# A Winograd convolution with batch norm and SiLU: the order of its opening written out as a table

## The chip, the cores and the metric

The kernel runs on one core of a Trainium2 chip. The metric is the device time of one execution in microseconds. Three timed runs of the kernel before gave 185.06, 185.35 and 185.8 us, median 185.35. PE is the matrix engine (TensorE), DVE the vector engine, ACT the scalar engine, POOL GpSimd, SP the engine that here only issues loads and stores.

## The reference

A 1-d convolution of width 3 over the sequence, per-channel scale and shift, and SiLU. x is [2, 2048, 1024] in bf16, w is [3, 1024, 1024].

```python
xp = jnp.pad(x, ((0, 0), (1, 1), (0, 0)))
y = sum(jnp.einsum('bsc,cd->bsd', xp[:, k:k + 2048, :], w[k]) for k in range(3))
inv_std = 1.0 / jnp.sqrt(var + 1e-5)
y = (y - mean) * (g * inv_std) + b
return y * jax.nn.sigmoid(y)
```

## The kernel before

**The method.** Six neighbouring outputs are computed from eight inputs with eight products instead of eighteen: the eight inputs are transformed to eight *points* (numbers 0 to 7; 0 is "point 0", 7 is "point inf"), each point is multiplied by a transformed weight, and the eight products are combined to six outputs. Points 0 and 7 take taps 0 and 2 of w as they are; points 1 to 6 take `u`, sums and differences of the taps, that POOL makes (lines 157 to 248): even sums `e0` to `e2`, then `u0` (points 1, 2), `u1` (3, 4), `u2` (5, 6). POOL's order is: the scales of the batch norm, which need the parameters `prm` (`scales`, line 239), the even sums and scaled copies (`evens`, 199), a doubled middle tap and the six `u` of output chunk 0 (`left`, 206), then those of output chunk 1.

**Transform jobs.** x comes in 2 sequences x 8 blocks of 128 channels ("chunks"), 512 KB each, the first two in two halves. A block has 16 frames. A *job* is six or four frames: as many matmuls of 168 columns (line 296: the x frame is the stationary side, the constant matrix `rm` the moving one) into two PSUM banks, and then one copy of 1008 or 672 elements per partition to `T_sb` by ACT (310) or DVE (312). A block is 6 + 6 + 4 frames. Each sequence has one *short* job more for its tail (eight matmuls of 48 columns, line 285, from the load `xl`).

**Products.** For each of 8 output chunks and 2 sequences there is a `Unit`: 8 points x 8 input chunks = 64 matmuls of 342 columns (line 340; in the first unit 470), copies on ACT and combines on DVE (356), SiLU on ACT (361), a store. The first unit (`First`, output chunk 0, sequence 0) uses banks 0 to 3 and mixes its products with the jobs of sequence 1: points 0, 7, 1, 3, 2 and 4, one point after the other, over 8 input chunks each. Points 0 and 7 are copied out to `kept`; point 1 is copied to `p`, point 2 is added in the same bank, and three combines make `sd`.

**The order of the work.** All engines execute in the order in which the program names their instructions. While the program is built, a small model keeps a `clock` per engine and estimated landings (lines 79 to 107, `landed`, `matmuls`, `busy`). The jobs of sequence 0 come first, all of them; `keep_busy` (99) adds filling matmuls where the model sees a gap (five of them, line 106). Then a loop (589) takes either the next job of sequence 1 or the next product of the first unit, by which one the model lets start first. Each job takes the pair of banks that is free first (`place`, 265): (4,5), (6,7), (2,3), for sequence 0 (0,1) as well. `ends` picks ACT or DVE for each copy (302, 479).

**Queues.** SP issues, in order: first halves of x blocks 0 and 1, the tail `xl`, x block 2, taps 0 and 2 of w, blocks 3 to 7, tap 1, the second tail, sequence 1's eight blocks, the next weights. ACT issues `rm`, the two second halves and `prm` (line 560, 8 KB in 128 pieces of 64 bytes). The loads of blocks 6 and later wait for one of six buffers.

Of the kernel before, what the change touches and what calls it, by code (L numbers as in the profile page):

```python
# [18 lines left out]
WARM_AT = 7000.0  # L19
FILL = 9000.0  # L20
# [3 lines left out]


@with_exitstack
def kernel(
# [50 lines left out]

    clock = {"pe": 4150.0, "act": 3700.0, "dve": 1500.0, "pool": 7000.0, "dma": 2300.0}
    cost = {"act": (0.833, 170.0), "dve": (1.042, 155.0), "pool": (2.0, 80.0)}  # L80

    def ends(e, size, ready):
        return max(clock[e], ready) + cost[e][0] * size + cost[e][1]

    def busy(e, size, ready=None):
        clock[e] = ends(e, size, clock["pe"] + 250.0 if ready is None else ready)
        return clock[e] + 100.0

    def landed(nbytes):
        left = nbytes  # L90
        slow = max(0.0, 6100.0 - clock["dma"]) * 300.0
        at = min(left, slow)
        clock["dma"] += at / 300.0 + (left - at) / 410.0
        return clock["dma"] + 300.0

    def matmuls(cols):
        clock["pe"] += cols / (2.34 if clock["pe"] > WARM_AT else 1.18)

    def keep_busy(until, bank):


        z = zeros.bitcast(BF16)
        n, gap, left = (192, 200.0, 100.0) if clock["pe"] < FILL else (384, 900.0, 600.0)
        if clock["pe"] + gap < until:
            while clock["pe"] + left < until:
                nc.tensor.matmul(ps[:, bank, 0:n], lhsT=z[:, 0:P], rhs=z[:, 0:n], start=True, stop=True)  # L106
                matmuls(n)

    xt, xt_at, raw, raw_at = {}, {}, {}, {}
    small, small_at = {}, {}  # L110

    def load_small(bi):
        t = xlpool.tile([P, CT * P], BF16, name="xl")
        nc.sync.dma_start(out=t[0:LROWS], in_=xl[bi])
        small[bi], small_at[bi] = t, landed(LROWS * CT * P * 2)

    def load_x(bi, ct, parts=1):
        t = xpool.tile([P, NF, P], BF16, name="xw")
        xt[bi, ct], xt_at[bi, ct] = t, []
        step = NF // parts  # L120
        for q in range(parts):
            s = slice(q * step, (q + 1) * step)
            (nc.scalar if q else nc.sync).dma_start(out=t[:, s], in_=x[bi, ct, :, s])
            at = landed(P * step * P * 2)
            xt_at[bi, ct] += [at] * step

    def load_w(dc, taps):
# [7 lines left out]
        for k in taps:  # L135
            raw_at[dc, k] = landed(P * CT * P * 2)
# [52 lines left out]
    def pool(n=1):  # L189
        clock["pool"] += n * 2130.0  # L190
        return clock["pool"]

    u_at = {}

    def prepare_first(dc):
# [3 lines left out]
        def evens():  # L199
            clock["pool"] = max(clock["pool"], raw_at[dc, 0], raw_at[dc, 2])  # L200
# [3 lines left out]
            pool(4)  # L204

        def left():
            clock["pool"] = max(clock["pool"], raw_at[dc, 1])
            double_w(dc, nc.gpsimd)
            pool(0.5)
            for q, i in ((0, 0), (1, 0), (0, 1), (1, 1), (2, 0), (2, 1)):  # L210
                transform_w(dc, q, (i,))
                u_at[1 + 2 * q + i] = pool()
# [39 lines left out]
    t_at, bank_free = {}, {}  # L252

    class Jobs:


        def __init__(self, bi):
            self.bi = bi
            self.todo = [(ct, f, min(6, NF - f)) for ct in range(CT) for f in range(0, NF, 6)]
            self.todo.insert(6, (None, 0, 0))  # L260

        def __bool__(self):
            return bool(self.todo)

        def place(self):

            ct, f, nf = self.todo[0]
            slots = [(4, 5), (6, 7), (2, 3)]
            if not self.bi:
                slots += [(0, 1)]  # L270
            slot = min(slots, key=lambda s: max(bank_free.get(k, 0.0) for k in s))
            at = small_at[self.bi] if ct is None else xt_at[self.bi, ct][f + nf - 1]
            return slot, max([at] + [bank_free.get(k, 0.0) for k in slot])

        def do(self):
            slot, at = self.place()
            clock["pe"] = max(clock["pe"], at)
            bank = slot[0]
            ct, f, nf = self.todo.pop(0)
            T = T_sb[self.bi]  # L280
            if ct is None:
                size, count, slot = CT * NJ * LAST, CT, slot[:1]
                src = ps[:, bank, 0:size].rearrange("p (c j n) -> p c j n", j=NJ, n=LAST)
                for c in range(CT):
                    nc.tensor.matmul(
                        src[:, c], lhsT=small[self.bi][0:LROWS, c * P:(c + 1) * P], rhs=rm[0:LROWS, :, 0:LAST],
                        start=True, stop=True,
                    )
                src = src.rearrange("p c j n -> p (c j) n")
                dst = T[:, :, :, NT:NB].rearrange("p c j n -> p (c j) n")  # L290
            else:
                size, count = nf * NJ * WT, nf
                per = nf // 2
                src = ps[:, bank:bank + 2, 0:per * NJ * WT].rearrange("p b (f j n) -> p b f j n", f=per, j=NJ)
                for q in range(nf):
                    nc.tensor.matmul(  # L296
                        src[:, q // per, q % per], lhsT=xt[self.bi, ct][:, f + q], rhs=rm, start=True, stop=True
                    )
                src = src.rearrange("p b f j n -> p j b f n")
                dst = T[:, ct, :, f * WT:(f + nf) * WT].rearrange("p j (b f n) -> p j b f n", b=2, f=per)  # L300
            matmuls(size)
            e = min(("act", "dve"), key=lambda k: ends(k, size, clock["pe"] + 250.0))
            done = busy(e, size)
            for k in slot:
                bank_free[k] = done
            if ct is None or f + nf == NF:
                for c in range(CT) if ct is None else (ct,):
                    t_at[self.bi, c] = max(done + 50.0, t_at.get((self.bi, c), 0.0))
            if e == "act":
# [14 lines left out]
    class Unit:  # L324
# [20 lines left out]
        def copy(self, q, dst=None, by=None):  # L345
# [6 lines left out]
            busy("act", self.hi - self.lo)  # L352
            return dst

        def combine(self, out, in0, scalar, in1, op1=ALU.add):
            nc.vector.scalar_tensor_tensor(out=out, in0=in0, scalar=scalar, in1=in1, op0=ALU.mult, op1=op1)  # L356
            busy("dve", (self.hi - self.lo) * (2 if len(out.shape) > 2 else 1))

        def silu(self, rows, src):
# [5 lines left out]
            busy("act", (self.hi - self.lo) * (2 if len(src.shape) > 2 else 1))  # L365
# [69 lines left out]
    class First(Unit):  # L435
# [3 lines left out]
        def __init__(self, dc, bi):  # L439
# [14 lines left out]
        def at(self):  # L454

            j, q, _, ct = self.todo[0]
            u = raw_at[self.dc, 0 if j == 0 else 2] if j in (0, NJ - 1) else u_at[j]
            if q == 2 and jobs[1]:
                return float("inf")
            return max(u, t_at[self.bi, ct], bank_free.get(q, 0.0))  # L460

        def do(self):
            at = self.at()
            j, q, add, ct = self.todo.pop(0)
            clock["pe"] = max(clock["pe"], at)
            if j == 0 or j == NJ - 1:
                lhsT = raw[self.dc][:, 0 if j == 0 else 2, ct]
            else:
# [3 lines left out]
                start=not add and ct == 0, stop=ct == CT - 1, skip_group_check=add,  # L472
            )
            matmuls(NB)
            if ct == CT - 1:
                bank_free[q] = self.behind(j, q)

        def out_of(self, q, dst, by=1.0):
            e = min(("act", "dve"), key=lambda k: ends(k, NB, clock["pe"] + 250.0))
            if e == "act":  # L480
# [3 lines left out]
            return busy(e, NB)  # L484

        def behind(self, j, q):
            b0, b1 = self.bank[:2]
            sd = self.sd
            if j == 0 or j == NJ - 1:
                return self.out_of(q, self.kept[:, j and 1])  # L490
            if j in (1, 3, 5):
                self.p = getattr(self, "p", {})
                self.p[j] = cpool.tile([P, NB], FP32, name="pc")
                return self.out_of(q, self.p[j], 4.0 if j == 3 else 1.0)
            if j == 2:
                at = self.out_of(q, sd[:, 0])
                self.combine(sd[:, 1], b1, 1.0, self.kept[:, 0])
                self.combine(sd[:, 2], self.p[1], 2.0, b1, ALU.subtract)
                at = max(at, clock["dve"])
                self.combine(sd[:, 3], sd[:, 2], 1.0, self.kept[:, 1])  # L500
                return at
            if j == 4:
                self.combine(b1, b0, -2.0, self.p[3])
                for t, a, s in zip(self.t, (-0.0125, -0.05, -0.2), (sd[:, 1:3], sd[:, 0:3:2], sd[:, 0:4:3])):
                    self.combine(t, self.low, a, s)
                return clock["dve"]
            return clock["dve"]
# [50 lines left out]
    load_x(0, 1, 2)  # L558
    load_small(0)
    nc.scalar.dma_start(out=prm, in_=prm_in)  # L560
# [13 lines left out]
    scales()  # L574
# [137 lines left out]
```

## Time and profile before

| what | us |
|---|---|
| median of the timed runs | 185.35 |
| the profiled execution | 185.1 |
| its span (first to last instruction) | 183.0 |
| around the span | 2.1 |
| PE busy | 175.1 |
| DVE busy | 152.1 |
| POOL busy | 141.6 |
| ACT busy | 108.8 |

The span is what the trace shows; the 2.1 us around it lie outside the trace. Times in rows of the trace count from the start of the span. In a row of the order of time, the first number is the start, the second the length, `x38` the number of instructions, and the bracket the idle time before it with what ended it. In the rows of stretches, the columns are PE, PEld (weight loads, which overlap), DVE, ACT and POOL busy time, the granted TensorE clock, the DMA share and GB/s. In the chain of waits a row is start, length, engine, tile and line.

### The profile page before, as it was taken

How to read it: one execution, taken by the hardware profiler on the slowest of the kernel's cores; microseconds unless marked ns; L12 is line 12 of the kernel's file. 1: busy time of each engine (PE TensorE's matmuls, PEld its weight loads, DVE VectorE, ACT ScalarE, POOL GpSimd, SP SyncE). 2: the span in 40 equal slices, each digit the busy share in tenths (PEclk: the TensorE clock that was granted, in tenths of full speed). 3: DMA queues.
4: the chain of work that ended last, by engine and by line, in shares of the span. 5: the costliest groups of instructions: out<-in, count | busy, mean ns of one | idle time of the engine just before them, and what ended most of it. 6: DMA issues, size and time to landing. Idle time of an engine off the chain costs nothing.

```text
span 183.0 us, 3476 instructions
## 1 busy us (share of the span) xinstructions
PE 175.1 (96%) x1371; PEld 125.1 (68%) x1371; DVE 152.1 (83%) x192; ACT 108.8 (59%) x174; POOL 141.6 (77%) x77
## 2 busy tenths in 40 slices
PE   7988899999999999999999999999999999999992
PEld 5876778766666666666666666666666666668891
DVE  0479577899978999999998999887998899766690
ACT  3789688846754565455545654564547454564773
POOL 2199999999999779999999999999999976000000
PEclk9999999999999999999999999999999999999997
DMA  5999991080308130543055304630302020203042
GB/s 177 370 415 372 412 416 77 19 326 4 129 0 260 46 129 0 136 171 129 0 113 192 129 0 79 225 129 2 123 9 114 15 101 33 91 38 126 6 180 80
DMA packets 7200, 24.58 MB, mean 134 GB/s; under 512 B 1072, under 2 KB 1456, under 8 KB 7184
## 3 DMA queue, kind: packets, MB, share of 16 engines
q1 hardware_dynamic: 6464, 23.73, 35.7%
q10 hardware_dynamic: 720, 0.64, 1.1%
q8 instruction: 10, 0.16, 0.4%
q14 instruction: 6, 0.05, 0.1%
HBM read 14.93 MB, written 9.44 MB: 133 GB/s over the span
## 4 chain that ended last, share of the span: by engine, by line
PE 62%; DVE 24%; DMA 7%; issue 2%; ACT 2%; DVEq 0%; ACTq 0%
PE ps L340 54%; DMA xw<-in_x_dram 7%; DVE ps L356 7%; DVE t L356 6%; PE ps L296 5%; DVE e L165 5%; PE ps L470 2%; DVE T_sb L312 2%; DVE sd L356 2%; DVE f L356 2%; ACT T_sb L310 1%; ACT yh L361 1%; PE ps L106 0%; ACTq L68 0%; DVEq L701 0%
## 5 line engine op out<-in xcount | busy, mean ns | idle before, releaser
L340 PE MATMUL ps<-T_sb,u 128*128 128x342 bf16 (+2 forms) x768 | 109.7, 298 | 0.0
L340 PEld LDWEIGHTS <-u 128*128 128x128 bf16 x768 | 72.5, 97 | 32.7
L172 POOL TENSOR_TENSOR u<-e,w1x 128x1024 bf16<-128x1024 f32 x32 | 69.3, 2189 | 3.9 <-DVE e L165 3.7
L340 PE MATMUL ps<-T_sb,wch 128*128 128x342 bf16 (+2 forms) x256 | 39.8, 299 | 0.5 <-DVE ps L356 0.4
L172 POOL TENSOR_TENSOR u<-e,wch 128x1024 bf16<-128x1024 f32 x16 | 38.8, 2439 | 0.5
L356 DVE SCALAR_TENSOR_TENSOR t<-ps,sd 128x684 f32<-128x684 f32 (+2 forms) x49 | 37.5, 819 | 0.6
L361 ACT ACTIVATE yT<-ps,beta,scale 128x342 bf16<-128x342 f32 (+1 forms) x42 | 29.2, 728 | 11.4 <-PE ps L340 11.4
L312 DVE CAST T_sb<-ps 128x1008 bf16<-128x1008 f32 (+2 forms) x22 | 22.6, 1066 | 11.7 <-PE ps L296 11.6
L340 PEld LDWEIGHTS <-wch 128*128 128x128 bf16 x256 | 24.2, 97 | 11.8 <-issue 1.2
L349 ACT COPY pc<-ps 128x342 f32<-128x342 f32 (+2 forms) x32 | 13.6, 425 | 30.4 <-PE ps L340 30.3
L310 ACT CAST T_sb<-ps 128x1008 bf16<-128x1008 f32 (+1 forms) x28 | 24.1, 892 | 5.5 <-PE ps L296 5.1
L356 DVE SCALAR_TENSOR_TENSOR ps<-ps,t 128x684 f32<-128x684 f32 (+2 forms) x32 | 26.5, 829 | 0.5
L165 DVE SCALAR_TENSOR_TENSOR e<-wch 128x1024 f32<-128x1024 bf16 x12 | 26.8, 2237 | 0.0
L296 PE MATMUL ps<-rm,xw 128*128 128x168 bf16 x256 | 23.4, 243 | 2.6 <-DMA xw<-in_x_dram 2.1
L296 PEld LDWEIGHTS <-xw 128*128 128x128 bf16 x256 | 20.2, 100 | 6.0 <-DMA xw<-in_x_dram 3.5
L356 DVE SCALAR_TENSOR_TENSOR ps<-ps,pc 128x342 f32<-128x342 f32 (+2 forms) x34 | 16.8, 495 | 8.5 <-PE ps L340 6.1
L159 POOL TENSOR_TENSOR e<-wch 128x1024 f32<-128x1024 bf16 x8 | 18.9, 2366 | 0.1
L361 ACT ACTIVATE yT<-t,beta,scale 128x684 bf16<-128x684 f32 x15 | 14.4, 959 | 0.0
L356 DVE SCALAR_TENSOR_TENSOR t<-ps,t 128x684 f32<-128x684 f32 (+2 forms) x17 | 13.9, 817 | 0.0
L349 ACT COPY sd<-ps 128x342 f32<-128x342 f32 (+2 forms) x16 | 6.8, 428 | 10.3 <-PE ps L340 9.7
L351 ACT ACTIVATE pc<-ps 128x342 f32<-128x342 f32 (+2 forms) x16 | 7.0, 438 | 8.9 <-PE ps L340 5.3
L356 DVE SCALAR_TENSOR_TENSOR sd<-pc,ps 128x342 f32<-128x342 f32 (+2 forms) x17 | 8.2, 483 | 4.5 <-ACT sd L349 4.4
(41 smaller groups left out, 66.2 us busy)
## 6 DMA issues: line engine op xcount, KB each, us to landing
out_dram<-yT SPq DMA_DIRECT2D x15, 576.0 KB, 2.8
xw<-in_x_dram SPq DMA_DIRECT2D x14, 512.0 KB, 7.5
wch<-in_w_dram SPq DMA_DIRECT2D x7, 768.0 KB, 5.6
wch<-in_w_dram SPq DMA_DIRECT2D x3, 256.0 KB, 4.9
xw<-in_x_dram SPq DMA_DIRECT2D x2, 256.0 KB, 3.6
xw<-in_x_dram ACTq DMA_DIRECT2D x2, 256.0 KB, 4.7
out_dram<-yh SPq DMA_DIRECT2D x1, 256.0 KB, 2.1
out_dram<-yh SPq DMA_DIRECT2D x2, 128.0 KB, 1.7
```

What stands on the lines that cost most here:

```text
L159: nc.gpsimd.tensor_tensor(sums[dc, q], a, b, op=ALU.add)
L165: nc.vector.scalar_tensor_tensor(out=e, in0=f, scalar=4.0, in1=h, op0=ALU.mult, op1=ALU.add)
L172: nc.gpsimd.tensor_tensor(wts[dc, q][:, i], sums[dc, q], o, op=(ALU.add, ALU.subtract)[i])
L296: nc.tensor.matmul(src[:, q // per, q % per], lhsT=xt[self.bi, ct][:, f + q], rhs=rm, start=True, stop=True)
L310: nc.scalar.copy(dst, src)
L312: nc.vector.tensor_copy(dst, src)
L340: nc.tensor.matmul(self.bank[q], lhsT=lhsT, rhs=T_sb[self.bi][:, ct, j, nsl], start=not add and ct == 0, stop=ct == CT - 1, skip_group_che ...
L349: nc.scalar.copy(dst, self.bank[q])
L351: nc.scalar.mul(dst, self.bank[q], by)
L356: nc.vector.scalar_tensor_tensor(out=out, in0=in0, scalar=scalar, in1=in1, op0=ALU.mult, op1=op1)
L361: nc.scalar.activation(self.yT[:, rows, self.y0:self.y0 + self.hi - self.lo], src, ACT.Silu, bias=beta[:, dc:dc + 1], scale=scale[:, dc:dc ...
L470: nc.tensor.matmul(self.bank[q], lhsT=lhsT, rhs=T_sb[self.bi][:, ct, j, :], start=not add and ct == 0, stop=ct == CT - 1, skip_group_check ...
```

## The change

The model that chose the order is taken out, with `keep_busy`, `place` and `ends`. In its place stands a table: each token is a job with its banks (A: 4,5; B: 6,7; C: 2,3; D: 0,1) and its copying engine (a: ACT, d: DVE), a short job (`s`), filling matmuls (`z5`) or a number of products of the first unit.

```diff
+BANKS = {"A": 4, "B": 6, "C": 2, "D": 0}
+ORDER = (
+    "Aa Ba Cd Da Ad Ba s2d z5 Dd Ba Ad Ca Bd Aa Dd Ca Aa Bd Ca Dd Aa Bd Ca 5 Ad 1 Bd Ca 5 Aa Cd 2 Ba "
+    "3 Aa Cd Ba 7 s4d Ca Bd Aa 4 Ca 1 Bd Aa 3 Ca 2 Ad Ba 2 Ca 2 Bd Aa 2 Ca 2 Ad Ba 2 Ca 3 Ba 1 Aa 1"
+)
+COPIES = {0: "d", 7: "a", 1: "d", 3: "d", 2: "d", 5: "a"}
...
-    jobs = [Jobs(0), Jobs(1)]
-    while jobs[0]:
-        slot, ready = jobs[0].place()
-        keep_busy(ready, slot[0])
-        jobs[0].do()
...
+    second = list(prepare_second(1))
+    second.pop(0)()
+    jobs, unit = Jobs(), First(0, 0)
+    for token in ORDER.split():
...
+        elif token[0] == "s":
+            jobs.do_short(int(token[1]), token[2])
+        elif token[0] in BANKS:
+            jobs.do(BANKS[token[0]], token[1])
         else:
-            unit.do()
+            for _ in range(int(token)):
+                unit.do()
+    for f in unit.later:
+        f()
+    while unit.todo[0][0] != 6:
+        unit.do()
+    second.pop(0)()
```

Points 0 and inf are now taken together, chunk by chunk (0 and 7 of chunk 0, then of chunk 1), and the first eleven of their sixteen products stand among the last jobs of sequence 0, behind chunk 6 and between chunk 7's jobs; the other five among chunk 0 of sequence 1. The other points follow as before. The combines behind points 2 and 4 are put off to the end of the table (`later`), and ACT's scaled copy of the next weights (`second.pop(0)`, which stood between jobs) behind them:

```diff
-            self.todo = [
+            self.todo = [(j, q, False, ct) for ct in range(CT) for j, q in ((0, 0), (NJ - 1, 1))] + [
                 (j, q, add, ct) for j, q, add in (
-                    (0, 0, False), (NJ - 1, 1, False), (1, 1, False), (3, 0, False), (2, 1, True), (4, 0, True),
-                    (5, 2, False), (6, 2, True),
+                    (1, 1, False), (3, 0, False), (2, 1, True), (4, 0, True), (5, 2, False), (6, 2, True),
                 ) for ct in range(CT)
             ]
```

Point inf is added to twice point 1 straight from the bank, before point 2 is added there; the later combine then subtracts the bank:

```diff
+            if j == 1:
+                self.combine(sd[:, 3], b1, 2.0, self.kept[:, 1])
             if j == 2:
-                at = self.out_of(q, sd[:, 0])
-                self.combine(sd[:, 1], b1, 1.0, self.kept[:, 0])
-                self.combine(sd[:, 2], self.p[1], 2.0, b1, ALU.subtract)
-                at = max(at, clock["dve"])
-                self.combine(sd[:, 3], sd[:, 2], 1.0, self.kept[:, 1])
-                return at
+                self.out_of(j, q, sd[:, 0])
+                self.later += [
+                    lambda: self.combine(sd[:, 1], b1, 1.0, self.kept[:, 0]),
+                    lambda: self.combine(sd[:, 2], self.p[1], 2.0, b1, ALU.subtract),
+                    lambda: self.combine(sd[:, 3], sd[:, 3], 1.0, b1, ALU.subtract),
+                ]
```

Of the first unit's copies out of PSUM, those of points 0, 1, 2 and 3 are now on DVE, those of 5 and inf on ACT (before: one on DVE, five on ACT). Of the 48 jobs and two short ones DVE now copies 20 and ACT 30 (before 22 and 28); of sequence 1 DVE has seven of six frames and the short one. And the parameters are loaded third on SP's queue instead of fourth on ACT's, with the scales named right behind:

```diff
     load_x(0, 0, 2)
     load_x(0, 1, 2)
+    nc.sync.dma_start(out=prm, in_=prm_in)
     load_small(0)
-    nc.scalar.dma_start(out=prm, in_=prm_in)
+    scales()
```

More of the change, by code (lines that the diff above doesn't have):

```diff
@@ L76 @@
     nc.vector.memset(dummy, 0.0)
[L79 to L110, printed above, removed]
+    xt, raw, small = {}, {}, {}
     def load_small(bi):
@@ new lines, in do_short @@
+        def do_short(self, bank, eng):
+            bi = self.short.pop(0)
+            src = ps[:, bank, 0:CT * NJ * LAST].rearrange("p (c j n) -> p c j n", j=NJ, n=LAST)
+            for c in range(CT):
+                nc.tensor.matmul(
+                    src[:, c], lhsT=small[bi][0:LROWS, c * P:(c + 1) * P], rhs=rm[0:LROWS, :, 0:LAST],
+                    start=True, stop=True,
+                )
+            dst = T_sb[bi][:, :, :, NT:NB].rearrange("p c j n -> p (c j) n")
+            self.out(dst, src.rearrange("p c j n -> p (c j) n"), eng)
```

131 lines of the change are left out of this document (30 added, 101 removed).

## Prediction

> **What bounds the kernel now.** I read the page first, then the busy time by stretches, then the chain of waits, then the order of time of TensorE (PE) from 10 to 37 us.
>
> ```profile
> span 183.0 us, 3476 instructions
> PE 175.1 (96%) x1371; PEld 125.1 (68%) x1371; DVE 152.1 (83%) x192; ACT 108.8 (59%) x174; POOL 141.6 (77%) x77
> ...
> L296 PE MATMUL ps<-rm,xw 128*128 128x168 bf16 x256 | 23.4, 243 | 2.6 <-DMA xw<-in_x_dram 2.1
> ```
>
> PE is the bound, but its busy time overlaps itself: the last row says 243 ns for a transform matmul, and below the next one starts after 72. So dead time must be found by counting starts. The stretches show where to look:
>
> ```profile
> 10.00:15.00 5.00, 4.21 (x53) 3.57 (x51) 4.33 (x4) 4.54 (x7) 4.48 (x8) 1.00 1.02 409
> 15.00:20.00 5.00, 3.71 (x47) 3.27 (x45) 4.11 (x5) 3.74 (x5) 4.85 (x3) 1.00 1.04 377
> 20.00:25.00 5.00, 5.00 (x60) 4.12 (x58) 3.02 (x4) 3.93 (x6) 5.00 (x4) 1.00 1.03 410
> ...
> 35.00:40.00 5.00, 5.00 (x38) 3.39 (x36) 4.93 (x7) 2.83 (x6) 4.92 (x3) 1.00 0.74 275
> ...
> 45.00:50.00 5.00, 5.00 (x37) 3.36 (x35) 4.95 (x7) 3.88 (x7) 4.92 (x3) 1.00 0.29 118
> ```
>
> The reader sees PE (first column) short of 5.00 before 20 us while the DMA share is 1.0: the loads of x hold it there. After 20 us PE is full. The chain of waits gives PE's price per matmul, and shows how the rest of the run goes:
>
> ```profile
> 26.12 0.89 PE ps L296 x10
> ...
> 27.00 0.58 PE ps L470 x4
> 27.58 0.43 PE ps L296 x6
> ...
> 50.39 4.82 PE ps L340 x32
> ...
> 79.71 93.97 PE ps L340 x664
> ```
>
> A product (342 columns) costs 0.58/4 = 0.145 us, a transform matmul (168 columns) 0.43/6 = 0.072 us. The chain passes from DVE to PE at 50.39 and for the last time at 79.71, and from there it is 664 products at 93.97/664 = 0.1415 us, so whatever PE gains by then reaches the end. Now PE itself:
>
> ```profile
> 10.70 3.29 PE L296 MATMUL ps<-rm,xw 128*128 128x168 bf16 x38 [0.48 <-DMA xw<-in_x_dram]
> 14.23 3.50 PE L296 MATMUL ps<-rm,xw 128*128 128x168 bf16 x42 [0.23 <-DVE T_sb L312]
> 19.00 1.04 PE L296 MATMUL ps<-rm,xw 128*128 128x168 bf16 x12 [1.27 <-DMA xw<-in_x_dram]
> ...
> 24.94 0.45 PE L470 MATMUL ps<-T_sb,wch 128*128 128x342 bf16 x2
> 25.47 1.53 PE L296 MATMUL ps<-rm,xw 128*128 128x168 bf16 x16
> ...
> 35.11 1.18 PE L470 MATMUL ps<-T_sb,u 128*128 128x342 bf16 x7
> ```
>
> The row at 14.23 holds the last 42 transform matmuls of sequence 0 (128 in all). After it PE has nothing that it may do until block 0 of sequence 1 lands: 1.27 us idle at 19.00, which is the largest hole in the run. At 25.47 it lost another 25.47 - 24.94 - 2x0.145 = 0.24 us to a PSUM bank that had not been emptied, and 0.22 inside that row to another (the chain has its last ten from 26.12, and the six before them need 0.43 of the 0.65). The last product of point 4 starts at 35.11 + 6x0.145 = 35.98, so ends its turn at 36.13.
>
> **The change part by part.**
>
> *Order table.* The work on PE is the same: 48 transform jobs, two short ones, 48 first products, and the same five filling matmuls. What moves is that 11 products of points 0 and inf now stand between the last jobs of sequence 0. They need T of chunks 0 to 5 and taps 0 and 2 of w:
>
> ```profile
> 1.61 0.42 SPq L114 DMA_DIRECT2D xl<-in_xl_dram  x1
> 2.08 0.42 SPq L123 DMA_DIRECT2D xw<-in_x_dram  x1
> 3.99 0.81 SPq L134 DMA_DIRECT2D wch<-in_w_dram  x2
> ```
> ```profile
> 2.12 0.45 ACTq L560 DMA_DIRECT2D prm<-in_prm_dram  x1
> ```
> ```profile
> wch<-in_w_dram SPq DMA_DIRECT2D x3, 256.0 KB, 4.9
> ...
> prm<-in_prm_dram ACTq DMA_DIRECT2D x1, 8.0 KB, 6.1
> ```
>
> The second tap is issued about 4.4 and takes 4.9, so both are in at 9.3. At 14.23 there are 26 matmuls to the end of chunk 6 (16.1), then 11 products (1.60) and chunk 7's 16 matmuls (1.16): 18.9, against 19.0 for the block that PE waits for. The bank waits inside the row at 14.23 (3.50 less the 0.17 by which a matmul's 243 ns outlasts its turn, less 42x0.072 = 0.3) may push it to 19.1. The hole is filled.
>
> From 19.0 on both orders are counts. Before: 128 matmuls 9.2, the short job 0.2, 48 products 6.96: 35.4; the trace says 36.13, so 0.7 was lost, 0.45 of it in the two bank waits. After: 37 products, 5.37, so 33.8; with the 0.25 that has no name kept, **34.05, or 2.1 us earlier**. If the bank waits stay as they are it is 1.6, if nothing is lost at all 2.3. I take **2.0**, since 0.1 may be carried past 19.0.
>
> That holds if nothing is late in the new order. Four covers:
>
> *Weights for points 1 to 4* come from POOL:
>
> ```profile
> 8.26 0.20 POOL L243 TENSOR_SCALAR sc<-prm 128x8 f32<-128x8 bf16 x1 [6.70 <-DMA prm<-in_prm_dram]
> ...
> 11.37 2.12 POOL L159 TENSOR_TENSOR e<-wch 128x1024 f32<-128x1024 bf16 x1
> ...
> 21.10 2.14 POOL L172 TENSOR_TENSOR u<-e,wch 128x1024 bf16<-128x1024 f32 x1
> ...
> 27.37 6.30 POOL L172 TENSOR_TENSOR u<-e,w1x 128x1024 bf16<-128x1024 f32 x3
> 33.63 2.12 POOL L159 TENSOR_TENSOR e<-wch 128x1024 f32<-128x1024 bf16 x1
> ```
>
> The first u is ready at 23.2. The table (Aa Cd 2 Ba 3 Aa Cd Ba) puts 32 transform matmuls (2.3) and 5 products (0.7) between 19.0 and the first product that wants it, so PE is there at 22.0. Unmoved, PE would stand 1.2 us. But POOL starts only when prm has landed (2.12 + 6.1 = 8.2), and then needs 11.37 - 8.26 = 3.1 us for the scales. *prm third on SP's queue* takes the place that xl had (issued 1.61):
>
> ```profile
> DMA to landing us min/median/max: 4.6/6.3/8.0
> ```
>
> These are xl's two loads; the smaller is the first, so it landed at 6.2. With prm at 6.2 or sooner the scales end by 9.3, as the second tap lands. POOL then starts 2.0 us earlier, and as it is busy without a break (5.00 of 5.00 above) all its u come 2.0 earlier: 21.2 against 22.0 wanted, then every 2.1 us (23.3, 25.4, 27.5) against about 24.5, 27.2, 30.7. Slack 0.8 at the first. SP's xl and x block 2 go out 0.42 later (one issue); a megabyte stands ahead of them in a stream at 409 GB/s, so nothing. ACT issues one DMA less before a first job that waits for PE anyway: nothing.
>
> *Blocks of x.* After 19.0 they land every 512 KB/410 GB/s = 1.28 us; PE reaches them in 1.6 to 1.9 us steps, so only the first is waited for. *Emptying the banks:*
>
> ```profile
> L310 ACT CAST T_sb<-ps 128x1008 bf16<-128x1008 f32 x17 | 16.9, 1001 | 5.2 <-PE ps L296 5.0
> ...
> L310 ACT CAST T_sb<-ps 128x672 bf16<-128x672 f32 x11 | 8.0, 725 | 0.3 <-PE ps L296 0.2
> ```
> ```profile
> 24.42 3.34 ACT L310 CAST T_sb<-ps 128x1008 bf16<-128x1008 f32 x4 [0.79 <-PE ps L296]
> ```
> ```profile
> 24.86 1.21 DVE L312 CAST T_sb<-ps 128x1008 bf16<-128x1008 f32 x1 [0.93 <-PE ps L296]
> 25.98 0.51 DVE L483 TENSOR_SCALAR kept<-ps 128x342 f32<-128x342 f32 x1
> ```
>
> (The first two rows group ACT's jobs from 4 to 37 us.) Of sequence 1 ACT has 9 jobs of six frames (1.00) and 8 of four (0.725) and one copy (0.5): 15.3 at most, and less what neighbours overlap, since two of each take 3.34 and not 3.45 in the row at 24.42, and with it 0.1 at best per job, 13.6 to 14.8. It can use 19.6 to 34.9, 15.3 us. DVE has 7 jobs (1.21), the short one (no more than a job), four copies and a combine (0.5 each): 12.2. Both fit; ACT's margin is 5 to 10%. ACT's scaled copy of the next weights moves behind the last job, to about 35.5, and POOL wants it after one more e and two u, 31.6 + 2.1 + 4.2 = 37.9: nothing.
>
> *Point inf from PSUM.*
>
> ```profile
> 35.71 0.50 DVE L356 SCALAR_TENSOR_TENSOR sd<-ps,kept 128x342 f32<-128x342 f32 x1
> ...
> 36.66 1.67 DVE L356 SCALAR_TENSOR_TENSOR sd<-sd,kept 128x342 f32<-128x342 f32 x1
> ...
> 55.71 0.52 DVE L356 SCALAR_TENSOR_TENSOR ps<-ps,pc 128x342 f32<-128x342 f32 x1 [2.07 <-PE ps L340]
> ```
>
> The combine with both inputs in SBUF took 1.67; its two replacements each read PSUM, as the 0.50 row does. So 1.67 goes and 1.0 comes (bounds: 0.5 to 1.67 each, so -0.7 to +1.7 on DVE), with three more copies (0.51 each) taken from ACT. DVE is full from 35 to 50 and only at 55.71 waits for PE (2.07), so it matters whether it keeps up: its last job now is chunk 6's second, behind which PE has 20 transform matmuls and 7 products (2.45), so PE ends it at 31.6 and DVE is free for the combines at about 32.9 instead of 35.7, 2.8 earlier for a PE 2.0 earlier. Cost on the path: nothing. POOL's next weights move by the same 2.0 as PE's need.
>
> **Sum:** 185.1 (the profiled execution: 183.0 span and 2.1 around it) less 2.0 is 183.1. The median of the runs, 185.35, lies 0.25 above that execution; halfway between the two bases I forecast **183.2**. The bounds of the unknown terms (1.6 to 2.3, and the base) give 182.8 to 183.7.
>
> **The rivals.** A measurement of this kernel can tell about 0.5%, 0.93 us, from no change.
>
> *A. prm does not land early enough.* If it lands at 8.2 as now, u is ready at 23.2, PE stands 1.2 at 22.0, and the time is 184.3. For it: 6.1 us from issue to landing for 8 KB. Against: xl's 4.6 from the very place. The Trainium skill (DMA: Bandwidth & Descriptors, "Issuing engines are not separate DMA queues") says that loads from SP and ACT run on the same 16 engines and interleave, and another issuing engine saves only issue time; by that rule the new queue brings only the half microsecond of earlier issue. That half microsecond (2.12 to 1.61) worked out in rows: landing 7.7, u at 22.7, PE stands 0.7, 183.8. No row here parts the queue from the time of issue; but xl, issued 0.5 before prm, landed 2.0 before it, so a place in the stream is worth more than its issue time. I put A at 184.0, between the two.
>
> *B. Banks.* ACT's margin is 5 to 10%. If waits like the 0.24 and 0.21 recur four times instead of twice, 0.9 of the gain is gone: 184.0. For: a fixed engine per job can't give way. Against: points 0 and inf keep PE off the banks for 0.3 to 0.7 us between jobs.
>
> *C. PE's fixed order meets a late u: slower.* All that stands behind point 1's first seven products (the second short job and the 18 jobs of chunks 2 to 7) waits with them; before, the first products that need a u stand near 27 (the row at 27.00), 3.8 after it is ready. Price 1:1. The gain is gone when the first u comes at 22.0 + 2.0 = 24.0, and from 25.0 the kernel is over 0.5% slower; at 25.2 it would take 186.4. That needs prm at over 10, beyond every row but xl's second load, 8.0 us in the full stream. Against: 6.2.
>
> *D. It is given back.* PE comes 2.0 earlier but DVE's work, full from 35 to 53.6, does not; PE then waits at 50.39, and the time is 185.1. For: 4.95 of 5.00. Against: the 2.8 above.
>
> **How the numbers follow.** Forecast 0.66, better than its range 0.03, A 0.10, B 0.10, D 0.06, C 0.05. The range takes in the forecast's bounds, A and B: 182.6 to 184.4. Faster by over 0.5% (under 184.4): forecast, the better end, B and most of A, 0.87; within: D and the rest of A, 0.08; slower: C, 0.05.
>
> **What would show it.** In the profile after: at 19 PE's wait for x under 0.3 instead of 1.27; POOL's first e at about 9.3 instead of 11.37 and its first u at 21.2; no PE idle at 22; the last product of point 4 near 34 instead of 36; no combine of 1.67; the hole before PE's 50.39 no larger than now. An idle PE at 22 with the u as its releaser says A or C, many short ones released by ACT B, one near 48 released by DVE D.

## The result, and the profile after

The changed kernel takes 183.08 us (median of 5 runs, 182.91 to 183.24), the kernel before on the same chip 185.17 (5 runs, 184.89 to 185.80): 2.1 us less, ratio 0.988 (95% interval 0.986 to 0.990). The forecast was 183.2. The profiled execution took 183.18 us with a span of 181.3; the one of before had 185.1 and 183.0. The spans of the five runs after are 181.0 to 181.5. In several kernels below the spans spread less than the times (in run 1 182.9 to 183.5 against 184.72 to 186.12), so I use them beside the times. A few executions, whatever the kernel, show a granted clock of 0.991 or less instead of 0.994 or more and a span 1.5 to 2.4 us longer; four of the twelve of run 6 are such.

The head of the page, after:

```profile
span 181.3 us, 3481 instructions
PE 174.4 (96%) x1371; PEld 124.5 (69%) x1371; DVE 151.6 (84%) x194; ACT 108.7 (60%) x173; POOL 141.4 (78%) x77
```

PE's share is the same 96%, DVE and POOL do what they did. A page's head can't show a gain of this kind, since the work is unchanged and only PE's idle time went. The stretches (the first column of busy time is PE's) say where:

```profile
10.00:15.00 5.00, 3.68 (x45) 3.26 (x46) 4.05 (x5) 3.85 (x5) 4.85 (x3) 1.00 1.03 419
15.00:20.00 5.00, 4.97 (x57) 4.15 (x55) 4.65 (x5) 3.34 (x5) 4.85 (x5) 1.00 1.04 376
...
35.00:40.00 5.00, 5.00 (x37) 3.35 (x35) 4.45 (x7) 4.12 (x7) 5.00 (x3) 1.00 0.79 298
```

Between 15 and 20 us PE is now busy for 4.97 instead of 3.71. Between 10 and 15 it is busy for less than before (3.68 against 4.21): in this execution the blocks of x came later. From 35 to 40 DVE, 4.93 before, has 0.55 to spare. Now PE itself, in order of time:

```profile
11.10 3.20 PE L225 MATMUL ps<-rm,xw 128*128 128x168 bf16 x38 [1.15 <-DMA xw<-in_x_dram]
14.52 2.13 PE L225 MATMUL ps<-rm,xw 128*128 128x168 bf16 x26 [0.21 <-ACT T_sb L242]
...
18.54 0.89 PE L389 MATMUL ps<-T_sb,wch 128*128 128x342 bf16 x5
19.46 1.04 PE L225 MATMUL ps<-rm,xw 128*128 128x168 bf16 x12
...
22.59 1.18 PE L389 MATMUL ps<-T_sb,u 128*128 128x342 bf16 x7
...
34.55 1.48 PE L389 MATMUL ps<-T_sb,u 128*128 128x342 bf16 x9
```

Block 0 of sequence 1 is the row at 19.46. The bracket of 1.27 us that stood there is gone. A bracket shows idle time after the last matmul's modelled end, so I also count starts: five products from 18.54 need 5 x 0.145 = 0.72, which leaves 0.20 to 19.46; before, the same count gave 1.44 (the row at 14.23 ends its last turn at 14.23 + 3.50 - 0.17 = 17.56). The first products that want a u (22.59) wait for nothing, and the two bank waits near 25 to 26 are not there. They had carried no bracket before either, so here too the count of starts decides: from 22.59 to 34.55 it leaves no gap over 0.1 us, against 0.24 and 0.22. The first of the nine products at 34.55 is the last of point 4, so that point ends at 34.70, where it ended at 36.13: **1.43 earlier**.

The span is 1.7 shorter, so 0.3 more was gained behind this point. The chain of waits has the place:

```profile
48.12 0.80 DVE ps L287
48.96 123.01 PE ps L272 x864
```

Before, the chain passed from DVE to PE twice, at 50.39 and at 79.71. Now it does so once, and 864 products follow in one piece. By the count of starts a hole of 0.30 stood at 79.71; it is gone, and 1.43 + 0.30 = 1.73 is the span's difference. The hole at 48.96 is 0.33, as it was at 50.39.

POOL and DVE, in order of time:

```profile
6.08 0.20 POOL L204 TENSOR_SCALAR sc<-prm 128x8 f32<-128x8 bf16 x1 [4.52 <-DMA prm<-in_prm_dram]
...
9.91 2.12 POOL L131 TENSOR_TENSOR e<-wch 128x1024 f32<-128x1024 bf16 x1 [0.78 <-DMA wch<-in_w_dram]
...
19.64 2.13 POOL L144 TENSOR_TENSOR u<-e,wch 128x1024 bf16<-128x1024 f32 x1
...
53.55 4.22 POOL L144 TENSOR_TENSOR u<-e,wch 128x1024 bf16<-128x1024 f32 x2
```
```profile
26.72 0.50 DVE L287 SCALAR_TENSOR_TENSOR sd<-ps,kept 128x342 f32<-128x342 f32 x1
...
34.47 0.50 DVE L287 SCALAR_TENSOR_TENSOR sd<-sd,ps 128x342 f32<-128x342 f32 x1
...
56.77 2.08 DVE L137 SCALAR_TENSOR_TENSOR e<-wch 128x1024 f32<-128x1024 bf16 x1
```

prm is there at 6.1 instead of 8.2, and POOL then stands 0.78 for the second tap of w, which is what limits it now. The combine of 1.67 became two of 0.50.

### The profile page after: what moved, and what is told of

The parts are those of the page before. It is cut to its first block, busy times and chain, and to the rows that moved or that the text cites. A ratio compares the mean times of both kernels' runs of the same rounds, so it can differ in the third digit from the quotient of the medians.

```text
span 181.3 us, 3481 instructions
## 1 busy us (share of the span) xinstructions
PE 174.4 (96%) x1371; PEld 124.5 (69%) x1371; DVE 151.6 (84%) x194; ACT 108.7 (60%) x173; POOL 141.4 (78%) x77
## 4 chain that ended last, share of the span: by engine, by line
PE 85%; DVE 6%; DMA 5%; ACT 1%; issue 0%; ACTq 0%; DVEq 0%
PE ps L272 71%; PE ps L225 8%; DMA xw<-in_x_dram 5%; PE ps L389 5%; DVE ps L287 3%; DVE t L287 3%; ACT yh L291 1%; ACT T_sb L242 1%; ACTq L76 0%; DVEq L618 0%; PE ps L233 0%; DVE sd L287 0%; DVEq L287 0%
## 5 line engine op out<-in xcount | busy, mean ns | idle before, releaser
L242 ACT CAST T_sb<-ps 128x1008 bf16<-128x1008 f32 (+1 forms) x30 | 25.2, 884 | 6.9 <-PE ps L225 6.3
L244 DVE CAST T_sb<-ps 128x1008 bf16<-128x1008 f32 (+2 forms) x20 | 21.2, 1086 | 9.3 <-PE ps L225 8.6
```

Source lines behind the costliest of these rows:

```text
L242: nc.scalar.copy(dst, src)
L244: nc.vector.tensor_copy(dst, src)
```

## The experiments

Two theories stood at the start. **Mine**: the gain is the hole at 19, filled by products, and the move of prm is worth nothing by itself but is the cover that lets the new order run (u in time). **The rival**: the parts help separately, or the stream of x (which differs from one execution to the next) or point inf's combine makes the time. The table has all runs; a kernel's ratio is to the kernel before on the same chip.

| run | kernel | time, us (runs) | span, median | ratio (95%) |
|---|---|---|---|---|
| 1 | changed, prm back behind ACT's two halves of x | 184.89 (12) | 183.0 | 0.9985 (0.9959 to 1.0011) |
| 2 | before, prm third on SP | 185.13 (12) | 183.2 | 0.9994 (0.9960 to 1.0029) |
| 3 | changed, products 0/inf behind block 0's first jobs | 184.66 (12) | 182.8 | 0.9971 (0.9943 to 0.9999) |
| 4 | changed, old combine of point inf | 183.24 (4) | 181.3 | 0.9883 (0.9838 to 0.9928) |
| 5 | changed, again | 183.11 (6) | 181.25 | 0.9875 (0.9834 to 0.9915) |
| 6 | changed, prm third on ACT | 184.03 (12) | 182.25 | 0.9939 (0.9903 to 0.9976) |
| 7 | changed, small load behind block 0 | 183.05 (6) | 181.0 | 0.9873 (0.9836 to 0.9909) |
| 8 | changed, one more copy on POOL | 184.00 (7) | 182.2 | 0.9921 (0.9891 to 0.9951) |
| 9 | changed, DVE's first e with one input | 182.97 (6) | 181.15 | 0.9868 (0.9836 to 0.9900) |
| 10 | run 8, DVE's first e with one input | 183.56 (6) | 181.75 | 0.9899 (0.9873 to 0.9925) |
| 11 | run 1, DVE's first e with one input | 184.26 (6) | 182.5 | 0.9930 (0.9906 to 0.9954) |
| 12 | run 7, DVE's first e moved | 183.70 (6) | 181.8 | 0.9918 (0.9900 to 0.9935) |

The kernel before took 185.23, 185.34, 185.37 and 185.19 beside runs 1 to 4, 5 to 8, 9 to 11 and 12, with median spans of 183.3 to 183.4.

### Run 3: the hole back

```diff
-"... Aa Bd Ca 5 Ad 1 Bd Ca 5 Aa Cd 2 Ba 3 Aa Cd Ba 7 ..."
+"... Aa Bd Ca Ad Bd Ca Aa Cd 8 Ba 8 Aa Cd Ba 7 ..."
```

> The changed kernel with the 16 products of points 0 and inf all behind the first two jobs of sequence 1 (8, one job, 8), none among the last jobs of sequence 0. Theory (the gain is the filled hole at 19): PE waits about 1.2 us there again and the time is 184.2 to 184.5. Rival (the gain is in the bank waits of 25 to 26 us, which are gone in either order): the time stays at 183.1 to 183.4.

Measured: 184.66. PE in order of time:

```profile
16.97 1.42 PE L225 MATMUL ps<-rm,xw 128*128 128x168 bf16 x16 [0.45 <-ACT T_sb L242]
19.32 1.04 PE L225 MATMUL ps<-rm,xw 128*128 128x168 bf16 x12 [0.93 <-DMA xw<-in_x_dram]
...
35.93 1.47 PE L389 MATMUL ps<-T_sb,u 128*128 128x342 bf16 x9
```

The hole stands at block 0 again, 0.93 of it as a bracket, and 0.45 more at 16.97, where PE without products runs into a bank that ACT hasn't emptied. The second is not a price of its own: the landing of block 0 sets 19.32, and with a free bank PE would only have stood longer there. The price is the eleven products that now stand behind block 0. From its start to the end of point 4 it is 35.93 + 0.145 - 19.32 = 16.76, in the changed kernel 34.70 - 19.46 = 15.24: 1.52 more. The time is 1.5 to 1.6 more, a little over the 184.2 to 184.5 that I expected. So where the products stand is worth about three quarters of the 2.1 us. The rival falls: near 25 to 26 the count of starts shows no bank wait here either, and still the time was lost.

### Runs 1, 2 and 6: prm's place

Run 2 puts prm third on SP in the kernel before:

```diff
+    nc.sync.dma_start(out=prm, in_=prm_in)
     load_small(0)
-    nc.scalar.dma_start(out=prm, in_=prm_in)
```

> The kernel before with prm third on SP's queue and nothing else. Theory: no difference, 185.2 (within 0.3), since the order of before reaches the first u 3.8 us after it is ready; POOL starts about 1.5 us earlier all the same. Rival (prm's 64-byte pieces ahead of xl and block 2 hold the x stream): the wait for block 0 of sequence 1 ends at 19.4 instead of 19.0 and the time is 185.6.

Measured: 185.13 against 185.23, no difference, although POOL starts its first e at 9.59 instead of 11.37. The old order has no use for an early u at its first products. Two smaller effects cancel in its profile: PE's wait for block 0 ends at 19.33 instead of 19.00, as the rival had it, and the hole of 0.30 at 79.71 is gone (runs 8 to 11 show why); the span is 183.0 in both. Run 1 is the changed kernel without the move:

> The changed kernel with prm back on ACT's queue, behind the second halves of x blocks 0 and 1; all else as changed. Theory (the early prm is what keeps the new order from waiting for u): prm lands near 8.2, POOL's first u near 23.2, PE stands 0.6 to 1.2 us before the first product of point 1 at about 22.5, so 183.7 to 184.3 us. Rival (moving prm is worth nothing, the order alone brings the gain): 183.1, PE idle there under 0.2. If prm third on SP's queue was also what made the x stream 0.45 later in the changed kernel, x block 3 lands at 10.7 here and block 0 of sequence 1 at 19.0; otherwise at 11.1 and 19.4.

Measured: 184.89, so 1.8 of the 2.1 us are lost, more than the expected 0.6 to 1.2. The profile of run 1 (its longest execution, span 183.5 against a median of 183.0), POOL and then PE:

```profile
8.92 0.20 POOL L204 TENSOR_SCALAR sc<-prm 128x8 f32<-128x8 bf16 x1 [7.36 <-DMA prm<-in_prm_dram]
```
```profile
20.34 1.04 PE L225 MATMUL ps<-rm,xw 128*128 128x168 bf16 x12 [0.32 <-DMA xw<-in_x_dram]
...
24.00 1.19 PE L389 MATMUL ps<-T_sb,u 128*128 128x342 bf16 x7 [0.36 <-ACT T_sb L242]
...
80.20 1.32 PE L272 MATMUL ps<-T_sb,wch 128*128 128x342 bf16 x8 [0.63 <-DVE ps L287]
```

prm came at 8.9. The wait for the first u is there (24.00; its releaser is named ACT, but POOL's first u ended at 23.9). But the largest of the three waits shown is one that no theory had: 0.63 at 80 us, behind DVE. Runs 8 to 11 go after it. The side question of the expectation, whether prm on SP is what makes x late, gets no answer: block 0 came at 20.34 here, later than both of the values named. Run 6 asks whether the queue or the place in it matters, with prm between ACT's two halves of x:

```diff
     load_x(0, 0, 2)
+    nc.scalar.dma_start(out=prm, in_=prm_in)
     load_x(0, 1, 2)
-    nc.sync.dma_start(out=prm, in_=prm_in)
```

> The changed kernel with prm back on ACT's queue, but third there, between the two halves that ACT loads of blocks 0 and 1 (so issued near 1.2 us instead of 2.1). Theory (the place in the stream, and with it POOL's start, decides, and the queue does not): prm lands by 6.5, POOL's first e at 9.9 as in the changed kernel, 183.1 (182.8 to 183.6; one half of block 1 goes out one issue later, which may cost up to 0.4). Rival (ACT's queue itself makes a small load late): prm lands after 8, POOL's first e at 11.4 or later, and the time is 184.9 as with prm behind both halves.

Measured: 184.03. POOL and then PE of run 6:

```profile
6.74 0.20 POOL L204 TENSOR_SCALAR sc<-prm 128x8 f32<-128x8 bf16 x1 [5.17 <-DMA prm<-in_prm_dram]
...
9.85 2.12 POOL L131 TENSOR_TENSOR e<-wch 128x1024 f32<-128x1024 bf16 x1
```
```profile
8.63 0.76 PE L225 MATMUL ps<-rm,xw 128*128 128x168 bf16 x8 [1.00 <-DMA xw<-in_x_dram]
```

On ACT's queue too prm is there by 6.7 and POOL starts at 9.85, as in the changed kernel, so in this trace the queue as such does not make the load late. The Trainium skill (DMA: Bandwidth & Descriptors, "Issuing engines are not separate DMA queues") says that loads started by different engines run on the same 16 DMA engines and interleave, and the trace agrees. The time is still 0.9 more than run 5's, and 0.7 more (183.85) over the eight executions with spans of 181.7 to 182.5; I had expected at most 0.4. The half of block 1 that goes out behind prm comes late: PE stands 1.00 at 8.63 for it and reaches the first product that wants a u at 23.06, 0.47 later than the changed kernel. The profiled execution loses no more than that (span 181.7); where the others lose the rest is not shown. So SP was the better queue for a reason that I had not given: third on ACT, prm holds up a half block that PE wants at once.

### Run 4: point inf

```diff
-            if j == 1:
-                self.combine(sd[:, 3], b1, 2.0, self.kept[:, 1])
...
-                    lambda: self.combine(sd[:, 3], sd[:, 3], 1.0, b1, ALU.subtract),
+                    lambda: self.combine(sd[:, 3], sd[:, 2], 1.0, self.kept[:, 1]),
```

> The changed kernel with point inf added as before: no combine behind point 1, and the last combine takes both inputs from SBUF. Theory (the combine is on no path): DVE's combine takes about 1.7 us again instead of two of 0.5, DVE's later waits for PE shrink, 183.1 within 0.2. Rival (DVE is close to the path, and its earlier start is what removed the 0.3 us hole at 79.7): that hole is back and the time is 183.4 to 183.8.

Measured: 183.24, the same as the changed kernel. DVE of run 4:

```profile
34.65 1.95 DVE L287 SCALAR_TENSOR_TENSOR sd<-sd,kept 128x342 f32<-128x342 f32 x1
```
```profile
34.10 4.49 POOL L144 TENSOR_TENSOR u<-e,wch 128x1024 bf16<-128x1024 f32 x2
```

The long combine is back, even longer, and DVE is merely later into waits that it has for PE anyway. Its length is not all work. POOL's first u of this pair takes 2.13, to 36.23, and the combine ends at 36.60, 0.37 later; in the kernel before the two ends are 37.96 and 38.33, again 0.37 apart. So the combine stands behind POOL's u, as DVE's e does in runs 8 to 11, and POOL's pair takes 4.49 instead of the changed kernel's 4.23. In this execution POOL had started its first e at 9.61 instead of 9.91, which covers those 0.26. This part of the change is worth nothing that these runs can tell.

### Runs 5 and 7: the stream of x

Run 5 is the changed kernel once more; run 7 has sequence 1's small load behind its block 0:

```diff
-    load_small(1)
-    for ct in range(CT):
+    load_x(1, 0)
+    load_small(1)
+    for ct in range(1, CT):
         load_x(1, ct)
```

> The changed kernel once more, on the chip of the next three, as their base: 183.1 (182.9 to 183.4). Theory: in its profile PE waits under 0.7 us for block 0 of sequence 1 near 19.4, in the measure in which the stream of x is late, has no wait at the first product that wants a u (22.6), none of the two waits for a bank near 25 to 26, and no hole near 80. Rival (what its first profile showed is that one execution's): a wait at 22 to 23 or a hole near 80 appears here.

> The changed kernel with sequence 1's small load xl (96 KB) behind its block 0 instead of ahead of it; the short job that uses it stands at 23.7. Theory (after the change the stream of x still holds PE for 0.20 to 0.63 us near 19.4 in the executions profiled so far): block 0 lands 0.3 to 0.9 earlier, that wait goes, and the time is 0.2 to 0.5 less than the changed kernel's on this chip, about 182.7. Rival (the 16 us stretch, not the bytes ahead of the block, sets its landing, or the gain meets u at 21.75): no difference, 183.1.

Measured: 183.11 and 183.05. Run 5 has a bracket of 0.43 for block 0 and none of the other holes. In run 7 PE, and then DVE:

```profile
18.89 1.04 PE L225 MATMUL ps<-rm,xw 128*128 128x168 bf16 x12
...
22.03 1.18 PE L389 MATMUL ps<-T_sb,u 128*128 128x342 bf16 x7
```
```profile
56.21 2.25 DVE L137 SCALAR_TENSOR_TENSOR e<-wch 128x1024 f32<-128x1024 bf16 x1
```

Block 0 is there in time, and PE is 0.5 ahead at 22.03. But the span's median is only 0.25 less, which these runs can't tell from none. DVE is 0.56 earlier at its e (56.77 in the changed kernel), which then takes 2.25 instead of 2.08, and a hole of 0.19 appears at 77.6. The gain was partly given back, at the place where run 1 had lost.

### Runs 8 to 11: what stands at 80 us

Theory: DVE's first e of the loop reads two inputs from SBUF and stands until POOL's running pair of u has ended; DVE then has no break up to 80 us, so what it loses there PE loses at 80. A late POOL would so cost twice. Run 8 makes POOL 1.1 late by one more copy:

```diff
     evens()
+    scaled(raw[0][:, 0], 4.0, nc.gpsimd)
     left()
```

> The changed kernel with one more scaled copy on POOL (1.04 us, its result unused) behind the three sums e, so each u comes about 1.1 us later. Forecast's slack at the first u was 0.8, the changed kernel's profile shows 22.6 - 21.75 = 0.85. Theory (a late POOL costs only past that slack at the first u, and then once more where DVE's e near 57 stands until POOL is done with its last u): PE waits 0.2 to 0.3 near 22.7, the hole near 80 comes back with 0.3 or less, 183.4 to 183.8. Rival (only the first u counts): 183.2 to 183.4. Rival (POOL's chain is on the path all along): 184.1 or more.

Measured: 184.00, 0.9 more than run 5 and over the range that I gave. PE, DVE and POOL of run 8:

```profile
19.41 1.04 PE L225 MATMUL ps<-rm,xw 128*128 128x168 bf16 x12 [0.36 <-DMA xw<-in_x_dram]
...
22.72 1.19 PE L389 MATMUL ps<-T_sb,u 128*128 128x342 bf16 x7
...
78.89 1.32 PE L272 MATMUL ps<-T_sb,wch 128*128 128x342 bf16 x8 [0.60 <-DVE ps L287]
```
```profile
56.91 2.83 DVE L137 SCALAR_TENSOR_TENSOR e<-wch 128x1024 f32<-128x1024 bf16 x1
```
```profile
54.44 4.22 POOL L144 TENSOR_TENSOR u<-e,wch 128x1024 bf16<-128x1024 f32 x2
```

At the first u PE lost 0.18 (by the count of starts), about the 1.1 less the slack of 0.85; the rest is the hole at 78.9, 0.77 by that count, larger than I had put it. The two make up the 0.9, so the trace speaks against the second rival, POOL on the path all along, though its 184.1 is only 0.1 away. e ends at 56.91 + 2.83 = 59.74, POOL's pair of u at 54.44 + 4.22 = 58.66: 1.08 apart. The same difference in the other kernels, from their rows, here the kernel before (DVE, then POOL):

```profile
58.60 1.95 DVE L165 SCALAR_TENSOR_TENSOR e<-wch 128x1024 f32<-128x1024 bf16 x1
```
```profile
55.26 4.22 POOL L172 TENSOR_TENSOR u<-e,wch 128x1024 bf16<-128x1024 f32 x2
```

60.55 less 59.48 is 1.07. In the changed kernel it is 58.85 less 57.77, again 1.08. So e doesn't take 1.95, 2.08 or 2.83 of work; it takes 1.1 behind the end of u. In run 2 POOL's pair had ended 1.0 before e began (DVE, then POOL):

```profile
58.93 1.22 DVE L165 SCALAR_TENSOR_TENSOR e<-wch 128x1024 f32<-128x1024 bf16 x1
```
```profile
53.71 4.21 POOL L172 TENSOR_TENSOR u<-e,wch 128x1024 bf16<-128x1024 f32 x2
```

There e took 1.22, and the hole near 80 was gone. The Trainium skill (SBUF — State Buffer, "Who interferes with whom") says that a DVE instruction with two SBUF inputs contends with a GpSimd instruction that reads SBUF, and that the ports they share are an exclusive lock, where the order of issue decides who blocks. The trace agrees with it in each of these cases.

Runs 9 to 11 shorten that one operation; their kernels leave out tap 0's term of that one sum:

```diff
+        if (dc, q) == (2, 1):
+            nc.vector.tensor_scalar(e, f, 4.0, 0.0, op0=ALU.mult, op1=ALU.add)
+        else:
             nc.vector.scalar_tensor_tensor(out=e, in0=f, scalar=4.0, in1=h, ...)
```

> The changed kernel with one DVE operation altered: the first e of the loop (4 times tap 2 plus tap 0, output channels 256 to 383), which near 57 us read two SBUF inputs, reads one (tap 0's term is left out of that sum, so those output channels are not the reference's). Control for the next two. Theory (with POOL early, this operation's stand behind POOL's u costs nothing on the path): it takes about 1 us or less instead of 1.7 to 2.1, and the time stays at 183.1 (182.9 to 183.4). Rival (it costs even here): 182.8 or less.

> The kernel with one more scaled copy on POOL, with the same one DVE operation reading one SBUF input (tap 0's term left out of that sum). Theory (the 0.77 hole at 78.9, thus nearly all of the 0.9 that POOL's extra copy cost, is DVE's e standing until POOL's u has ended, 1.08 us before e's own end in every profile so far): the operation no longer ends 1.08 behind POOL's u, the hole goes, and the time is 183.2 to 183.4, with the 0.18 at the first u left. Rival (DVE is simply full there, or the hole has another cause): 183.9 to 184.1 with the hole.

> The kernel with prm back behind ACT's two halves of x, with the same one DVE operation reading one SBUF input (tap 0's term left out of that sum). It took 184.9 with the whole operation. Theory (its loss of 1.75 was 0.3 to 0.5 at the first u, 0.8 at the hole near 80, and the rest a late stream of x): 184.0 to 184.3, with no hole at 80. Rival (the loss is all at the first u and in the stream): 184.8 to 185.0.

Measured: 182.97, 183.56 and 184.26. DVE, POOL and PE of run 10, then PE of run 11:

```profile
57.05 2.31 DVE L138 TENSOR_SCALAR e<-wch 128x1024 f32<-128x1024 bf16 x1
```
```profile
54.58 4.23 POOL L147 TENSOR_TENSOR u<-e,wch 128x1024 bf16<-128x1024 f32 x2
```
```profile
22.86 1.19 PE L392 MATMUL ps<-T_sb,u 128*128 128x342 bf16 x7 [0.55 <-POOL u L147]
...
72.46 5.97 PE L275 MATMUL ps<-T_sb,u 128*128 128x342 bf16 x40
78.51 1.32 PE L275 MATMUL ps<-T_sb,wch 128*128 128x342 bf16 x8
```
```profile
18.96 1.04 PE L228 MATMUL ps<-rm,xw 128*128 128x168 bf16 x12
...
23.36 1.19 PE L392 MATMUL ps<-T_sb,u 128*128 128x342 bf16 x7 [1.10 <-POOL u L147]
```

One part of the expectation fell: with one input the operation still stands behind POOL. It is 2.31 us long here, 2.27 in run 11, and 1.31 in run 9, where I had put it at 1 or less. But it ends at 59.36, 0.55 after u (58.81), and 0.54 to 0.55 after u in runs 9 and 11 as well, so half a microsecond sooner than with two inputs. The hole at 78.5 is 0.25 by the count of starts (the forty products from 72.46 need 5.80), 0.52 less than in run 8, and the time is 0.44 less; since the hole did not close, 183.56 lies above the 183.2 to 183.4 that I expected. In run 11 against run 1 the hole goes from 0.80 to 0.20, and the time is 0.63 less. (These pairs ran on different chips, on which the kernel before took 185.23 to 185.37, so the times differ by more than the chips do, but the holes are the surer measure.) In the control, run 9, the time stays (0.1 less, inside the runs' spread). So the hole near 80 is DVE's e behind POOL's u; that e with one input would not stand at all is refuted. The profiles of runs 8 and 10 also part the two waits for the first products. In run 10 block 0 of x was in time, and PE lost 0.71 at u by the count; in run 8, the same POOL but a late block, it lost 0.52 + 0.18 = 0.70. u sets the time there, and a late x is then free. In run 11, without the late x of run 1's profile, the wait for u is 1.10.

### Run 12: a try to beat both

Run 7, with DVE's first e behind one more combine, when POOL's u is about to end:

```diff
-also = also + [(1, lambda: idle(act_work)), (1, lambda: idle(dve_work))]
+also = also + [(1, lambda: idle(act_work)), (4, lambda: idle(dve_work))]
```

> The kernel with sequence 1's small load behind its block 0, and with the first e that DVE makes in the loop moved from ahead of three of unit 3's combines to behind two of them (the one into sd and the one into PSUM behind products of points 2 and 4 stand on either side of it), when POOL's u is about to end. Theory (in the first of these edits alone the 0.4 gained at 19.4 came back in part as a 0.19 hole at 77.6, DVE standing behind POOL's u): e takes 1.3 to 1.7 instead of 2.25, no hole near 78, 182.8 (182.6 to 183.0). Rival (the next e, or POOL's u that now start later, take it back): 183.0 to 183.3, with a wait at 70 to 80.

Measured: 183.70, on another chip than run 7; the spans, 181.7 to 182.3, lie above all of run 7's. DVE of run 12:

```profile
57.66 0.51 DVE L287 SCALAR_TENSOR_TENSOR sd<-pc,ps 128x342 f32<-128x342 f32 x1 [0.94 <-ACT sd L281]
58.09 1.22 DVE L137 SCALAR_TENSOR_TENSOR e<-wch 128x1024 f32<-128x1024 bf16 x1
...
62.12 2.67 DVE L137 SCALAR_TENSOR_TENSOR e<-wch 128x1024 f32<-128x1024 bf16 x1
```

e now takes 1.22, as planned, and the plan still fails. DVE waits 0.94 for ACT where e used to stand: that place had been idle time. POOL's next u, which need this e, start later (59.48 against 58.63 in run 7), and the next e stands behind them for 2.67 instead of 2.25. The hole at 78.5 grew to 0.62. That is the rival of the expectation, and the time lies beyond even its range. Not all of it is the edit's: PE's start behind the hole is 0.85 later than in run 7's profile, of which 0.42 was there at block 0 already (19.31 against 18.89). No run beat the changed kernel by more than the runs can tell.

## Why the prediction was right

The time (2.1 less against a forecast of 2.0 less) came out by the mechanism that the prediction named. By its own steps:

- **The hole at 19.0, filled by 11 products: right.** No bracket at 19.46, "under 0.3 instead of 1.27". Run 3 puts the products back and with them 1.5 us.
- **Count from 19.0, 34.05 for the end of point 4 and 2.0 earlier: right in length, shifted in place.** From block 0's start to the end of point 4 it is 34.70 - 19.46 = 15.24, against a forecast of 34.05 - 19.0 = 15.05 and 36.13 - 19.00 = 17.13 before. The start was 0.46 late, as block 0 came late, so at point 4 the profile shows 1.43 and not 2.0. Whether prm's new place makes block 0 late is open: with prm third on SP it starts at 19.3 to 19.5 in seven profiles of eight that issue x as the changed kernel does (19.0 in the eighth, run 10), with prm behind ACT's two halves at 19.00 (before), 18.96 (run 11) and 20.34 (run 1). That the medians still differ by 2.1 is in part luck: 0.30 came from a hole that the forecast had not counted, and the profile from which the forecast started was a quick one (span 183.0, its runs elsewhere 183.3 to 183.4), for which no trace here has the cause.
- **Bank waits of 0.45: gone**, as the value taken (2.0, with 0.1 kept back) had it. The forecast gave no reason why they would go, and which part of the table did it was not tested by itself. Rival B fell: ACT, 4.96 of 5.00 busy from 30 to 35 us, never made PE stand there.
- **prm third on SP: right.** It came at 6.1 (forecast 6.2). POOL's first e began at 9.91 and not at 9.3, since the second tap of w, which the forecast had in at 9.3, came 0.6 later. About half of that is issue: in this execution the two taps, which stand behind prm, go out from 4.30 instead of 3.99; the forecast had counted a later issue for xl and x block 2 alone. The first u ended at 21.77 instead of 21.2; PE wanted it at 22.59, so the slack of 0.8 held.
- **Rival A: its mechanism was right, its price too low.** The wait for u alone was put at 1.2 and its time at 184.3 for prm at 8.2 (184.0 was the value taken, between this and the milder case). Run 11 shows that wait as 1.10 and 184.26, with 0.20 of the hole at 80 left in it. But run 1, which is the rival itself, took 184.9. The term left out was the second payment, 0.6 to 0.8 at 80 us, where DVE's e stands behind a late POOL's u. The forecast had said "POOL's next weights move by the same 2.0 as PE's need" and had looked no further than when the weights are wanted, not at whom POOL holds up while it makes them.
- **Cost of point inf on the path, nothing: right** (run 4).
- **Hole before 50.39 no larger: right**, 0.33 both times; rival D fell. What I had not foreseen is that the second hole, 0.30 at 79.71, would go. POOL's pair of u, behind which DVE's e stands, ends 1.71 earlier (57.77 instead of 59.48) and PE is only 1.43 earlier, so 0.28 of the hole closes. It is small, and it makes up for part of the late start.
- **Rival C, slower: did not occur.** Its direction is seen in runs 1, 8 and 11: PE's fixed order waits for a late u one to one past the slack.

## What to carry to other kernels

A hole on the bound engine is filled by work that is ready early, and the price is paid in cover: what the moved work used to hide must now be in time by itself, so move the small load that starts its producer too, and test that both moves are needed together. When a helper engine gets later, ask not only who waits for its result but whose instruction stands while it works; here the second cost appeared 56 us further on. And before moving an operation out of a stall, look whether its place was idle time anyway.

## What the runs showed of the hardware

- DVE's e (two inputs in SBUF, 1024 elements) took 1.22 us with POOL idle (runs 2 and 12) and up to 2.84 (run 1) with POOL's u running. It ended 1.07 to 1.08 us after the end of u in the kernel before, the changed one and runs 1 and 8. POOL is held too: its e beside the loop's third e (67.13 to 69.77 in the changed kernel) took 3.11 us instead of 2.12. As a tensor_scalar with one SBUF input DVE's e stood as well, and ended 0.54 to 0.55 after u in runs 9 to 11: one input alone did not free this operation from POOL. The Trainium skill (SBUF — State Buffer, "Who interferes with whom") says that tensor_scalar can enter modes that use both ports and then can contend; the runs agree so far, though they don't show the mode.
- prm's 8 KB were there at 5.7 to 6.6 us when issued third on SP at 1.62 (ten profiles), at 6.7 when issued third on ACT at 1.64 (run 6), and at 8.3 to 8.9 when issued fourth on ACT at 2.12 (the kernel before, runs 1 and 11). So half a microsecond of issue was worth some 2 us of landing here. The load pushed back by it pays: in run 6 PE stood 1.00 us for a half block.
